# Attention with a routed expert layer on one core: other places for two blocks' gathers and one batch's scatters in GpSimd's queue

## The chip, the cores and the metric

The kernel runs on one core of one Trainium2 chip. Its time is in device microseconds (us) for one execution, and lower is better. Engine names are those of the profile: PE is the matrix engine, DVE the vector engine, ACT the scalar engine, POOL is GpSimd, and SP only issues transfers.

## The reference

Attention with rotary positions over 8 batches of 8 heads, 576 tokens and 64 features is followed by a layer of eight experts, of which each token uses one:

```python
attn = softmax(rotate(q) @ rotate(k).T / 8);  x = (attn @ v) as [4608 tokens, 512]
logits = x @ w_gate + modality_bias[modality_id]
e_idx = argmax(logits, axis=1)
gate_w = softmax(logits)[arange(N), e_idx]
for e in range(8):
    mask = e_idx == e
    h = maximum(x[mask] @ w1[e], 0.0)                 # 512 -> 1024
    out[mask] = gate_w[mask, None] * (h @ w2[e])      # 1024 -> 512
```

All inputs are float32. w1 is [8, 512, 1024] and w2 is [8, 1024, 512].

## The kernel before

**Two parts.** The attention part goes through 32 pairs of heads (`n` = 0 to 31, four pairs to a batch). After the last pair of a batch, `xout(b)` stores the batch's 576 rows of `x` to the scratch tensor `X` in memory, `route(b)` finds each token's expert and its place among that expert's tokens, and `scatter(b, j)`, five indirect DMAs of POOL, writes the tokens' numbers and gate weights into the table `TAB` (line L694 in the profile). The expert part takes the tokens of `TAB` in blocks of 256 rows of one expert, called slots. Slots 0 to 7 hold full blocks from the first five batches, so they can begin while the attention of the last batches still runs; the slots after them wait for every batch.

**A slot's work.** `m_plan` reads the slot's expert and rows into registers, `m_ix` loads its piece of `TAB` as `ix` and `xi` (SP, L930 and L932). `m_gather(s, t, g)` is one indirect DMA of POOL that brings 128 pieces of 128 numbers of `X` into `XG[s % 2][:, t, g, :]` (L956); a slot has eight, four for each half `t`. The first one of a slot is preceded by the POOL instruction that makes its list of rows, `iy` (L948). `m_tr` transposes one half in place on DVE (L1001), `m_tre` splits it into a high part on ACT (L419, `HL<-XG`) and a remainder on DVE (L416, `HL<-XG,HL`). `m_hi` and `m_lo` split the weights in the same way (`W1H`, `W2H` on L419, `W1L`, `W2L` on L416); the loads of weights carry a condition and move data only where a slot's expert differs from the one before it. `m_l1` is the first matrix product (L1020, 96 matmuls to a slot in four groups), `m_l1e` takes it out of PSUM (L1029 on ACT, L1030 on DVE), `m_l2` is the second product (L1043, 24 matmuls to each half), its rows are scaled on ACT (L1046) and scattered to the output by POOL (L1048).

**What sets the order.** PE, ACT, DVE, POOL and, through the first part, SP take their instructions in the order in which the program emits them. Up to the start of the expert part this order comes from a list of jobs, each with a due time: a name's number in `EDGE` or `MOE`, plus 14.438 for every pair of heads, and the list is sorted by it. `MOE["rows"]` holds the due times of the 24 gathers of slots 0, 1 and 2 (eight each), `MOE["ix"]` those of `m_ix`, and `EDGE[27]["SC0"]` that of the first scatter of batch 6, the last batch but one. Jobs due later than `end` (25.0 in the last pair's time) are emitted after the PSUM of the attention part has been given up:

```python
    for s in range(3):
        for i in range(8):
            Z("rows", 8 * s + i, m_gather, s, i // 4, i % 4, AFTER.get((s, i)))
    end = MOE["end"]
    for f in (m_tr, m_tre):
        for t in range(2):
            J(end + 0.05, "moe", z, f, 1, t)
    J(end + 0.1, "moe", z, m_l2, 0, 0)
    jobs.sort(key=lambda t: t[:2])
    cut_ = ([t[0] > PER * z + end for t in jobs] + [True]).index(True)
```

Behind the cut therefore stand slot 1's two `m_tr`, its two `m_tre` and slot 0's first `m_l2`. `chain` goes on from there: slot 0's second `m_l2`, then for each slot its `m_l1`, the next slot's splits and `m_tr`, and its `m_l2`; slot 3's gathers are emitted at slot 1, and so on. Batch 7's routing steps are sprinkled through it by `one()`. An entry of `AFTER` makes a gather wait for a named matmul as well: `('l1', 0)` is the last matmul of slot 0's first product that has been emitted by then.

Each indirect DMA of POOL uses one of eight semaphores in turn and waits until the DMA eight places earlier has landed.

Of the kernel before, what the change touches and what calls it, by code (L numbers as in the profile page):

```python
# [149 lines left out]
        "A_FB": 13.315, "B_FB": 14.059, "AVA": 14.280, "RE": 14.638, "A_F3": 14.844, "B_F3": 15.844, "OTA": 16.826, "AVB": 19.635,  # L150
# [3 lines left out]
    },  # L154
# [41 lines left out]
    setdma=(-353.070, -199.654, -64.082, -129.156),  # L196
    consts=(28.166, 28.282),
    plan=(-34.727, 16.183, -5.857, -25.884),
    ix=(-13.525, 17.418, 11.679, 11.775),
    w1=(-33.501, -27.735, 15.231, -22.655),  # L200
    w2=(-4.011, 1.762, 12.647, -8.483),
    hi=(-22.046, 1.027, 19.870, 16.903),
# [5 lines left out]
    l1=(17.301, 17.002, 22.720, 21.734),  # L208
    l1e=(22.809, 22.869, 24.662, 24.647),
    w1n=(20.502, 24.643, 23.254, 22.825),  # L210
    place=(10.490, 11.490),
    rows=(5.189, -7.595, 2.778, 1.170, -0.984, 8.071, 5.429, 11.766, 24.719, 23.818, 21.468, 24.323, 19.920, 20.117, 22.957, 17.444,
        18.250, 23.228, 17.169, 21.813, 22.941, 24.907, 21.508, 22.829),
    pl=(-114.356, -102.856, -99.906, -88.406, -85.506, -73.956, -51.417, -48.907, -45.303),
    end=25.0,
)
AFTER = {(0, 3): (30, 'av', 0), (0, 4): (30, 'av', 0), (0, 5): (30, 'av', 1), (0, 6): (30, 'av', 1), (0, 7): (30, 'out', 1), (1, 0): ('l1', 0), (1, 1): ('l1', 0), (1, 2): ('l1', 0), (1, 3): ('l1', 0), (1, 4): ('l1', 0), (1, 5): ('l1', 0), (1, 6): ('l1', 0), (1, 7): ('l1', 0)}
PIN = "PE,Activation,DVE,Pool"


# [1 line left out]
def tile_attention_moe(ctx: ExitStack, tc: tile.TileContext, qk, v, mod, wg, mb, w1, w2, rope, cf, ci, out):  # L222
# [912 lines left out]
    def Z(nm, i, f, *a):  # L1135
        J(MOE[nm][i], "moe", z, f, *a)
# [208 lines left out]
```

## Time and profile before

| | us |
|---|---|
| three runs | 919.7, 922.65, 923.22 (median 922.65) |
| the profiled execution | 919.6 |
| its span, first to last instruction | 917.8 |
| PE busy | 859.2 (94% of the span) |
| DVE / ACT / POOL busy | 684.9 / 631.3 / 652.8 |
| matmuls of the expert part from the middle of it on, each slot | 11.20 (L1020) and 11.10 (L1043) |

Times inside the trace are counted from the span's start. In a timeline row the columns are the start, the duration, the engine, the line, the operation with its output and inputs, the count, and in square brackets the engine's idle time before it and what ended it. The granted clock (PEclk) is PE's clock as a share of full speed. The attention part fills the first half; the expert part's matmuls begin at about 469 us and run until the end.

### The profile page before, as it was taken

The page shows a single profiled execution, that of the slowest core. Times are in us where ns is not written, and L with a number is a line of the kernel's source. Part 1 is how long each engine was busy: PE and PEld are TensorE (multiplying, and loading weights), DVE is VectorE, ACT ScalarE, POOL GpSimd, SP SyncE. Part 2 cuts the span into 40 slices and gives each one's busy share as a digit, 9 for nine tenths or more (in the row PEclk, how much of TensorE's full clock was granted, in tenths as well). Part 3 has the DMA queues.
Part 4 walks back from the last instruction along what each step waited for, and adds up shares of the span by engine and source line. Part 5 has one row for each costly group of instructions (what it writes and reads, how often), then busy time and mean ns, then how long its engine had stood idle before and what let it go on. Part 6 is the DMA issues. An engine that isn't in the chain of part 4 may idle for free.

```text
span 917.8 us, 25894 instructions
## 1 busy us (share of the span) xinstructions
PE 859.2 (94%) x9760; PEld 718.8 (78%) x9760; DVE 684.9 (75%) x1516; ACT 631.3 (69%) x1291; POOL 652.8 (71%) x494
## 2 busy tenths in 40 slices
PE   3899999999999999989994899999999999999995
PEld 2776777777777777766683799999999999999995
DVE  7777888888888889877781878766666666666662
ACT  2987988888988988978761555655555555555552
POOL 4989888998889899985466866766666666666400
PEclk9999999999999999999997799999999999999998
DMA  8776768978798887957612921127525112511240
GB/s 270 198 216 159 233 183 204 193 206 202 162 232 184 209 184 206 218 146 195 179 16 38 233 86 41 56 80 236 201 93 185 58 47 93 185 46 38 85 159 15
DMA packets 82466, 136.91 MB, mean 149 GB/s; under 512 B 28795, under 2 KB 53517, under 8 KB 81308
## 3 DMA queue, kind: packets, MB, share of 16 engines
q1 hardware_dynamic: 71740, 114.08, 47.2%
q0 software_dynamic: 9248, 19.46, 7.1%
q8 instruction: 79, 1.29, 0.6%
q10 hardware_dynamic: 1344, 1.62, 0.6%
q14 instruction: 55, 0.45, 0.2%
HBM read 138.16 MB, written 19.51 MB: 172 GB/s over the span
## 4 chain that ended last, share of the span: by engine, by line
PE 50%; issue 2%; POOL 1%; DVE 1%; DMA 1%; ACT 1%; POOLq 0%; DVEq 0%; ACTq 0%
PE psH L1020 22%; PE psY L1043 21%; PE ps L542 3%; PE ps L459 2%; PE ps L482 1%; POOL XG L956 1%; PE ps L1020 1%; DMA TAB<-VAL,oi 1%; PE ps L577 0%; DMA XG<-X,iy 0%; POOL TAB L694 0%; ACT PH L419 0%; DVE HL L416 0%; ACT P L477 0%; DVE X L589 0%
## 5 line engine op out<-in xcount | busy, mean ns | idle before, releaser
L477 ACT ACTIVATE P<-sc,mn 128x576 f32<-128x576 f32 x288 | 219.6, 766 | 5.9 <-DVE mn L468 4.8
L468 DVE CUSTOM_DVE_ANT_1 sc<-ps,ZERO 128x576 f32<-128x576 f32 x288 | 206.5, 748 | 21.8 <-PE ps L459 9.3
L1020 PE MATMUL psH<-HL,W1H 128*128 128x256 f32 x1152 | 205.2, 281 | 15.9 <-ACT W1H L419 15.9
L956 POOL DMA_INDIRECT XG<-X,iy x148 | 178.8, 1208 | 50.1 <-issue 36.7
L1020 PEld LDWEIGHTS psH<-HL,W1H 128*128 128x128 f32 x1152 | 178.9, 190 | 17.9 <-ACT W1H L419 16.4
L459 PE MATMUL ps<-SW 64*128 64x288 f32 x960 | 169.0, 311 | 14.7 <-DMA SW<-HL 12.5
L459 PE MATMUL ps<-HL 64*128 64x288 f32 x960 | 169.5, 311 | 5.8 <-DVE mn L468 2.1
L1020 PE MATMUL psH<-HL,W1L 128*128 128x256 f32 x576 | 162.1, 281 | 0.5 <-DVE W1L L416 0.5
L416 DVE TENSOR_TENSOR W1L<-ST,W1H 128x1024 fp32r<-128x1024 f32 x76 | 90.2, 1221 | 81.7 <-ACT W1H L419 81.6
L459 PEld LDWEIGHTS ps<-SW 64*128 64x128 f32 x960 | 135.5, 189 | 19.2 <-DMA SW<-HL 13.1
L459 PEld LDWEIGHTS ps<-HL 64*128 64x128 f32 x960 | 135.7, 189 | 11.3 <-issue 5.7
L542 PE MATMUL ps<-PH,V 128*64 128x320 f32 (+1 forms) x1024 | 138.2, 412 | 3.4 <-ACT P L477 2.1
L1048 POOL DMA_INDIRECT out_dram<-sc,ix x36 | 43.7, 1213 | 115.9 <-ACT sc L1046 100.0
L482 PEld LDWEIGHTS ps<-idf,P 64*128 64x128 f32 x2624 | 96.3, 139 | 33.3 <-ACT P L477 12.4
L1043 PE MATMUL psY<-W2L,SW 128*128 128x512 f32 (+1 forms) x304 | 118.0, 388 | 0.0
L1043 PE MATMUL psY<-W2H,SW 128*128 128x512 f32 (+1 forms) x304 | 116.7, 384 | 0.0
L482 PE MATMUL ps<-idf,P 64*128 64x64 f32 x2624 | 108.9, 226 | 7.5 <-ACT P L477 3.5
L516 DVE COPY PH<-ps 128x512 f32<-128x512 f32 (+1 forms) x160 | 98.4, 630 | 17.4 <-PE ps L482 12.2
L1020 PEld LDWEIGHTS psH<-HL,W1L 128*128 128x128 f32 x576 | 109.5, 190 | 0.8 <-DVE W1L L416 0.8
L436 POOL TENSOR_TENSOR HL<-ST,HL 128x1152 fp32r<-128x1152 f32 x31 | 82.4, 2657 | 38.9 <-ACT HL L419 38.8
L542 PEld LDWEIGHTS ps<-PH,V 128*64 128x64 f32 x1024 | 69.5, 136 | 50.3 <-issue 5.2
L419 ACT ACTIVATE PH<-ps 128x512 f32<-128x512 f32 (+1 forms) x160 | 85.5, 551 | 33.4 <-PE ps L482 25.4
(200 smaller groups left out, 1578.3 us busy)
## 6 DMA issues: line engine op xcount, KB each, us to landing
ST<-in_moe_w_dram SPq DMA_DIRECT2D x152, 512.0 KB
ST<-in_qk_dram SPq DMA_DIRECT2D x62, 576.0 KB
SW<-HL SPq DMA_DIRECT2D x124, 216.0 KB
V<-in_v_dram SPq DMA_DIRECT2D x32, 256.0 KB
X<-X SPq DMA_DIRECT2D x8, 1024.0 KB
XG<-X,iy POOLq DMA_INDIRECT x148, 3.1
V<-in_v_dram SPq DMA_DIRECT2D x64, 16.0 KB
X<-XT SPq DMA_DIRECT2D x16, 64.0 KB
```

What stands on the lines that cost most here:

```text
L416: nc.vector.tensor_tensor(o, a, b, op=ALU.subtract)
L419: return nc.scalar.activation(o, i, AF.Copy, scale=scale)
L436: e.tensor_tensor(d["HL"][:, 1, o], a, d["HL"][:, 0, o].bitcast(F32), op=ALU.subtract)
L459: nc.tensor.matmul(ps[:, g, 0:288], t[:, wq, q0:q0 + P], t[:, wk, k0:k0 + 288], start=(m == 0), stop=(m == len(L) - 1))
L468: nc.vector.tensor_tensor_reduce(sc, d.pop(("S", u))[:, :, 0:288], ZERO.unsqueeze(2).to_broadcast([P, 2, 288]), 1.0, FMAX, ALU.add, ALU.mi ...
L477: nc.scalar.activation(p, sc.rearrange("p a b -> p (a b)"), AF.Exp, bias=mn, scale=-1.0, accum_out=d["sum"][:, u:u + 1])
L482: nc.tensor.transpose(ps[:, g, c:c + 64], src[r, k0:k0 + P], idf[r, r])
L516: mine.append((nc.vector.tensor_copy if g else acopy)(o, i).ins)
L542: i = nc.tensor.matmul(pa[hh * 64:hh * 64 + 64, 0:c1 - c0], d["V"][:, hh, kt, :], r, start=(kt == 0), stop=(kt == 4))
L956: inst = nc.gpsimd.indirect_dma_start(out=XG[s % 2][:, t, g, :], out_offset=None, in_=X.rearrange("n (i f) -> (n i) f", f=P)[0:rows], in_o ...
L1020: l1_[s] = nc.tensor.matmul(ps[:, i, :], w[:, c, f0:f0 + P], x[:, c, :], start=(m == 0), stop=(m == 11)).ins
L1043: nc.tensor.matmul(ps, hx[:, c, t * P:(t + 1) * P], x[:, c, h * w:h * w + w], start=(m == 0), stop=(m == 23))
```

## The change

The due times are changed, and eight waits are left out:

- Slot 1's eight gathers get the due times 17.36 to 17.43 in their order, so that they stand in one run behind the first two scatters of batch 5. They waited for matmuls of slot 0's first product; that wait goes (the eight entries of `AFTER`).
- Slot 2's eight gathers get 25.15 to 25.22, and batch 6's first scatter 25.30 in the last pair's time (83.052 in its own). All nine are then behind the cut, so they are emitted after slot 1's `m_tr` and `m_tre` and slot 0's first `m_l2`.
- Slot 1's `m_ix` goes from 17.418 to 17.300, so that it still stands ahead of its gathers.

```diff
-        "RK11": 71.745, "RK12": 78.963, "RK13": 82.481, "RK14": 82.519, "SC0": 82.645,
+        "RK11": 71.745, "RK12": 78.963, "RK13": 82.481, "RK14": 82.519, "SC0": 83.052,
...
-    ix=(-13.525, 17.418, 11.679, 11.775),
+    ix=(-13.525, 17.300, 11.679, 11.775),
...
-    rows=(5.189, -7.595, 2.778, 1.170, -0.984, 8.071, 5.429, 11.766, 24.719, 23.818, 21.468, 24.323, 19.920, 20.117, 22.957, 17.444,
-        18.250, 23.228, 17.169, 21.813, 22.941, 24.907, 21.508, 22.829),
+    rows=(5.189, -7.595, 2.778, 1.170, -0.984, 8.071, 5.429, 11.766, 17.360, 17.370, 17.380, 17.390, 17.400, 17.410, 17.420, 17.430,
+        25.150, 25.160, 25.170, 25.180, 25.190, 25.200, 25.210, 25.220),
...
-AFTER = {(0, 3): (30, 'av', 0), ..., (0, 7): (30, 'out', 1), (1, 0): ('l1', 0), ..., (1, 7): ('l1', 0)}
+AFTER = {(0, 3): (30, 'av', 0), ..., (0, 7): (30, 'out', 1)}
```

The order on PE, DVE and ACT is the same before and after. On POOL, in the stretch from batch 5's first two scatters to slot 0's second output scatter, the program has this before (`XG_76` is `XG[1]`, which slot 1 uses, `XG_75` is `XG[0]`, slot 2's; `TAB<-VAL,oi` is a scatter of routing results):

```order
L948 TENSOR_SCALAR iy<-xi,CF 128x8
L956 DMA XG_76<-X,iy 128x128
L956 DMA XG_75<-X,iy 128x128
L956 DMA XG_76<-X,iy 128x128 x2
L694 DMA TAB<-VAL,oi 41472x2
L956 DMA XG_76<-X,iy 128x128
L956 DMA XG_75<-X,iy 128x128 x2
L694 DMA TAB<-VAL,oi 41472x2
L956 DMA XG_75<-X,iy 128x128 x2
L956 DMA XG_76<-X,iy 128x128
L956 DMA XG_75<-X,iy 128x128
L956 DMA XG_76<-X,iy 128x128 x3
```

Ahead of these rows stand slot 2's `iy`, one gather of slot 2 and a scatter; behind them one scatter of batch 6, slot 2's last gather, the first output scatter, and batch 6's other four. The program after the change has this on POOL from the same place on:

```order
L948 TENSOR_SCALAR iy<-xi,CF 128x8
L956 DMA XG_76<-X,iy 128x128 x8
L694 DMA TAB<-VAL,oi 41472x2 x3
L683 CAST oi<-of 128x5
L1048 DMA out_dram<-sc,ix 4608x512
L948 TENSOR_SCALAR iy<-xi,CF 128x8
L956 DMA XG_75<-X,iy 128x128 x8
L694 DMA TAB<-VAL,oi 41472x2 x5
L1048 DMA out_dram<-sc,ix 4608x512
```

Slot 1's gathers now stand together and ahead of three scatters; slot 2's stand together behind slot 0's first output scatter. On SP the order of batch 7's `xout` and of slot 4's `m_ix` is exchanged; both stand ahead of the loads of slot 2's W1. The rows of the difference are:

```order
-L930 ISA
-L930 DMA ix<-TAB 128x4
-L932 ISA
-L932 DMA xi<-TAB 128x1x16
-L601 DMA X<-XT 64x8x32
 L599 DMA X<-X 128x2048
-L601 DMA X<-XT 64x8x32
+L601 DMA X<-XT 64x8x32 x2
+L930 ISA
+L930 DMA ix<-TAB 128x4
+L932 ISA
+L932 DMA xi<-TAB 128x1x16
```

So slot 4's `ix` and `xi` now come behind the stores of batch 7's rows of `X`.

More of the change, by code (lines that the diff above doesn't have):

```diff
@@ L216 @@
 )
-AFTER = {(0, 3): (30, 'av', 0), (0, 4): (30, 'av', 0), (0, 5): (30, 'av', 1), (0, 6): (30, 'av', 1), (0, 7): (30, 'out', 1), (1, 0): ('l1', 0), (1, 1): ('l1', 0), (1, 2): ('l1', 0), (1, 3): ('l1', 0), (1, 4): ('l1', 0), (1, 5): ('l1', 0), (1, 6): ('l1', 0), (1, 7): ('l1', 0)}
+AFTER = {(0, 3): (30, 'av', 0), (0, 4): (30, 'av', 0), (0, 5): (30, 'av', 1), (0, 6): (30, 'av', 1), (0, 7): (30, 'out', 1)}
 PIN = "PE,Activation,DVE,Pool"
```

## The prediction

> **What bounds the kernel now.** I read the page first, for the engine with the highest share and for the slices in which it drops.
>
> ```profile
> PE 859.2 (94%) x9760; PEld 718.8 (78%) x9760; DVE 684.9 (75%) x1516; ACT 631.3 (69%) x1291; POOL 652.8 (71%) x494
> PE   3899999999999999989994899999999999999995
> PEclk9999999999999999999997799999999999999998
> ```
>
> PE is the bound, and its one weak place past the beginning is around slices 21 to 23 of 23 us each, where its clock falls too. PE's timeline there has one hole, from the last matmul of slot 0 to the first of slot 1:
>
> ```profile
> 492.06 0.39 PE L1043 MATMUL psY<-W2L,SW 128*128 128x512 f32 x1
> 508.37 0.58 PE L1020 MATMUL psH<-HL,W1H 128*128 128x256 f32 x1 [15.92 <-ACT W1H L419]
> ```
>
> The chain that ended last says what fills it (start, duration, what):
>
> ```profile
> 498.23 2.56 DMA XG<-X,iy
> ...
> 500.92 0.72 DVE XG L1001
> ...
> 501.71 1.12 ACT HL L419
> 502.86 2.08 DVE HL L416 x2
> ...
> 507.26 1.06 ACT W1H L419
> 508.35 1.24 DVE W1L L416
> ...
> 509.63 8.15 PE psH L1020 x46
> ...
> 517.93 5.71 PE psH L1020 x48
> 523.64 11.10 PE psY L1043 x48
> 534.74 11.20 PE psH L1020 x96
> ```
>
> Slot 1's last gather is issued at 498.23 and landed at 500.8. Then come transposes, the split of the rows, and the split of the weights, which ACT and DVE do only behind the rows. ACT names W1H as the releaser, but that was late because the gathers were. From 523.64 PE goes in blocks of 11.1 and 11.2 without a hole, to the end, so whatever makes slot 1 start and run earlier is taken off the end in full as long as slot 2 is not late in its turn.
>
> A slower clock makes the hole dearer (columns: PE, PEld, DVE, ACT, POOL busy, granted clock, DMA share, GB/s):
>
> ```profile
> 392.28:395.69 3.41, 1.81 (x22) 1.25 (x20) 2.34 (x8) 0.95 (x3) 2.71 (x7) 1.00 0.56 161
> 395.69:399.10 3.41, 3.41 (x58) 2.61 (x56) 3.41 (x10) 2.82 (x6) 1.57 (x1) 1.00 0.01 5
> 491.26:494.68 3.42, 1.19 (x6) 0.63 (x4) 0.00 (x0) 0.00 (x0) 2.51 (x4) 1.00 0.37 32
> 494.68:515.16 20.48, 6.33 (x28) 6.03 (x29) 12.74 (x25) 8.90 (x13) 14.71 (x15) 0.50 0.57 100
> ```
>
> After 3.4 us in which PE was busy for 1.19, the clock is 0.50 until 515.16; after 3.4 us with 1.81 it stayed at 1.00.
>
> **The change, first part: slot 1's gathers.** POOL's rows from slot 2's list of rows on, some left out:
>
> ```profile
> 467.92 1.35 POOL L948 TENSOR_SCALAR iy<-xi,CF 128x8 int32<-128x8 int32 x1
> 469.54 1.09 POOL L956 DMA_INDIRECT XG<-X,iy  x1 [0.28 <-POOL iy L948]
> 470.94 5.23 POOL L694 DMA_INDIRECT TAB<-VAL,oi  x1 [0.31 <-issue]
> 476.27 0.27 POOL L948 TENSOR_SCALAR iy<-xi,CF 128x8 int32<-128x8 int32 x1
> ...
> 479.54 2.57 POOL L956 DMA_INDIRECT XG<-X,iy  x1 [0.30 <-issue]
> ...
> 485.05 1.03 POOL L956 DMA_INDIRECT XG<-X,iy  x1 [0.30 <-issue]
> ...
> 498.23 1.00 POOL L956 DMA_INDIRECT XG<-X,iy  x1 [0.30 <-issue]
> ```
>
> POOL is never idle here for more than the 0.3 between two DMAs: the gathers are late because slot 2's seven and three scatters stand among them, not because of the wait for matmuls. That wait I cost at nothing: it was over before POOL came to it. In the changed order the list made at 467.92 is slot 1's, and its eight gathers take the next eight DMA places, those at 469.54, 470.94 and so on to 485.05; the second `iy` (0.27 and its gaps) drops out between. The last one starts at 485.05 instead of 498.23, if two long durations stay where they are. They belong to the first of these DVE rows:
>
> ```profile
> 470.60 1.21 DVE L416 TENSOR_TENSOR W1L<-ST,W1H 128x1024 fp32r<-128x1024 f32 x1
> 471.73 1.21 DVE L416 TENSOR_TENSOR W2L<-ST,W2H 128x1024 fp32r<-128x1024 f32 x1
> ...
> 474.07 1.21 DVE L416 TENSOR_TENSOR W2L<-ST,W2H 128x1024 fp32r<-128x1024 f32 x1
> ...
> 478.88 2.34 DVE L416 TENSOR_TENSOR W2L<-ST,W2H 128x1024 fp32r<-128x1024 f32 x2
> ...
> 500.92 1.30 DVE L1001 STREAM_TRANSPOSE XG<-XG 128x512 f32<-128x512 f32 x2 [17.64 <-DMA XG<-X,iy]
> ```
>
> The DMA of 470.94 began during the first subtraction and ended at 476.17, 0.89 after the last (475.28); that of 479.54 ended at 482.11, 0.89 after 481.22. A DMA of POOL that starts while DVE subtracts takes its usual time only after it. DVE's order is unchanged and nothing ahead of these rows moves, so I keep both stalls. The Trainium skill (SBUF — State Buffer, section "Who interferes with whom") says that a DVE instruction with two SBUF inputs blocks a GpSimd instruction that reads SBUF, and also that descriptor generation was seen not to be stalled by `tensor_tensor`, since it writes. By the second sentence the gathers would run unstalled, which is the first rival below; the row with 5.23 agrees with the first one, because an indirect DMA reads its list.
>
> The eighth gather then lands here after:
>
> ```profile
> L956 POOL DMA_INDIRECT XG<-X,iy x15: 1003/1012/2567, 469.5 to 498.2; - x15
> ...
> DMA to landing us min/median/max: 2.6/2.8/4.9
> ```
>
> I take 2.6, the price of the row at 498.23 (2.56), since now no scatter stands among the eight; 4.9 is the other end. That is 487.65, so the second transpose starts at 487.8. The first one needs only the first four gathers, which are out by 478.9 and landed by about 482, before DVE is free (500.92 less its 17.64 of idle time, 483.3); its ACT part is done early as well. Before, both halves waited for the end. From the second transpose: 0.67 for it, ACT's high part 1.1, DVE's remainder 1.1 with about 0.1 between, so DVE is through at 490.75, and as before (504.94 to 508.37) PE's first matmul comes 3.43 later, at 494.2. ACT's scaling of slot 0's first half, which stands ahead of W1H on ACT, needs PE's 24 matmuls up to 486.9 (half of 11.10 before 492.45) and is no longer late. PE's hole becomes 492.45 to 494.2, 1.75 instead of 15.92.
>
> Before, slot 1's first product took 508.37 to 523.64, 15.27. At full clock it costs 1.24 for the first piece of W1L behind the first two matmuls, then 94 of 96 matmuls by the 11.20 row, 10.97, and 0.15 for batch 7's small matmuls in it (509.63 + 8.15 to 517.93): 12.36. It ends at 506.56. The gain is 523.64 − 506.56 = 17.1, of which 14.2 are the hole and 2.9 the clock.
>
> Is the clock safe? PE idles 1.75 and then up to 1 more for W1L, so its busy time in a stretch of 3.41 is between 0.9 and 1.7, between the two rows above (1.19 fell, 1.81 did not). A fall to 0.50 for one such stretch costs half of it, 1.7 at most. I take half of that, 0.8, and keep 0 and 1.7. The Trainium skill (TensorE: Matmul & The Clock Gate, "What's actually happening") puts the fall after one idle window of 3.4 us; by it there is no fall and the sum stays at 17.1. The row with 1.19 busy, where the clock fell, differs from a wholly idle window.
>
> **Second part: slot 2's gathers**, now behind slot 0's first output scatter, which waits for ACT. The cover is slot 1's 22 us of matmuls. For the price I take what POOL did beside the same DVE work before:
>
> ```profile
> 504.46 1.37 POOL L1048 DMA_INDIRECT out_dram<-sc,ix  x1 [2.38 <-ACT sc L1046]
> 506.14 1.00 POOL L694 DMA_INDIRECT TAB<-VAL,oi  x1 [0.30 <-issue]
> ...
> 518.74 1.01 POOL L956 DMA_INDIRECT XG<-X,iy  x1 [0.30 <-issue]
> ...
> L956 POOL DMA_INDIRECT XG<-X,iy x8: 1003/1408/2053, 514.1 to 526.2; - x8
> ...
> DMA to landing us min/median/max: 6.4/6.5/7.0
> ```
>
> The first DMA behind the output scatter started at 506.14, the eighth at 518.74, with an `iy` between, as in the new order. Everything there moves up by 14.2 with DVE, so the scatter runs from 490.3 (three routing scatters of 1.3 from 486.4 fill POOL until then), and the eighth gather starts at about 504.5. With the weight loads beside it, it lands after 6.4 to 7.0, at 511.5 at the latest. It has to land by:
>
> ```profile
> 527.93 1.26 DVE L1001 STREAM_TRANSPOSE XG<-XG 128x512 f32<-128x512 f32 x2
> ...
> 530.88 1.09 DVE L416 TENSOR_TENSOR HL<-XG,HL 128x512 fp32r<-128x512 f32 x1
> ```
>
> From transposes to split rows are 4.04. PE wants slot 2 at 506.56 + 11.10 = 517.66, so 513.6 is the limit and 2.1 are left. I cost it at nothing; if the cover is gone, this run is what is late next.
>
> **The rest.** POOL's queue holds the same instructions as before; what is put off are batch 5's last three scatters and batch 6's five, by up to 16, and only the table loads of slot 8 and later read them. Slot 0's second output scatter and slot 3's gathers come at about 513 and 515 to 528, the gathers nearly as before (514.1 to 526.2), while PE's need of slot 3 moves up to 540 (517.66 and one block of 22.3): landed by 535, 1 us before its limit of 536. On SP the exchange lets slot 4's two loads wait for DVE's last values of batch 7; their reader is POOL at about 530, so nothing.
>
> Sum: 17.1 less 0.8 is 16.3. From the profiled 919.6 that is 903.3; this execution lay 3.05 below the median of the three runs, and from 922.65 it is 906.35. I say 905, between the two.
>
> **The rivals.**
>
> 1. The gathers are not held by DVE (the stalled DMA of 470.94 slips through between subtractions). Each takes 1.31, the eighth starts by 478.7 and slot 1 is ready before PE is: no hole, all of 15.92 + 3.9 = 19.8 gone, 903 from the median. For it: the subtractions are separate instructions, and one handover that POOL catches frees up to 3.5; against it: the same DMA place waited through all of them.
> 2. Slot 2 is late. Eight gathers at the dearest of 2.05 + 0.3 end at 511, plus 7.0 is 518: PE stalls 4.5 and the clock falls for 1.7 or more. The gain is 10 to 11, the time 912. For it: the margin of 2.1; against it: the median 1.41 of such gathers.
> 3. The change doesn't reach PE: another input of W1H is as late as the gathers (the values of the last pair, which DVE takes behind the split rows). Then 919 to 922. Against it: POOL's rows without idle time, and DVE idle for 17.64 before its transposes, with nothing but the gathers to wait for.
> 4. Slower: slot 2's run, now behind the output scatter, makes a longer hole than the one removed. It decides from a landing later than 513.6 + 17.1 = 530.7, that is (530.7 − 7.0 − 492.2) / 7 = 4.5 from gather to gather; at 5 it would be 926. One row has that length (5.23), with subtractions back to back; of the eight of 514.1 to 526.2, beside the DVE work that it would meet, none took over 2.05.
>
> **How the numbers follow.** The forecast has 0.73, the rivals 0.10, 0.10, 0.04 and 0.03. About 0.5%, 4.6 us, is what a measurement of this kernel can tell from no change. The forecast's own range is 902.5 (17.1 off the profiled execution) to 909.5 (landing after 4.9 and a full fall of the clock, so 13.1 off the median). With rival 2 it reaches to 912.5, with the first to 900: 900 to 912.5. Faster by more than 0.5% takes the forecast and both first rivals, 0.92; rival 3 is the same, 0.05; slower 0.03.
>
> **What would show it.** Right: in the changed trace eight gathers in a row from 469.5 to about 486, with long ones at the second and fifth; transposes apart, at 483 and 488; PE's first `psH` at 494 and the next `psY` at 506 to 508; no hole before slot 2. Wrong: a hole ahead of slot 2's or slot 3's L1020 with gathers landing just before, or W1H on ACT still near 507.

## The result and the profile after

The changed kernel takes 908.13 us (median of four runs, 905.53 to 910.39) against 922.13 (four runs, 919.7 to 923.22) for the kernel before beside it: a ratio of 0.9851, with an interval of 0.9815 to 0.9887. That is 14.0 us less; forecast were 905 and a range of 900 to 912.5. The profiled execution took 909.4, its span is 907.6, against 919.6 and 917.8 before. Two more comparisons below, each on another chip, gave ratios of 0.9891 and 0.9825. The ratios leave out runs over 1.5% above the fastest of their kernel, which are six of the twelve of `ahead_timed` below and none of the others.

Shares and slices on the page hardly tell the two apart: PE has 2 us more busy time, 95% of a shorter span, and the dips of work and clock in slices 21 to 23 are gone.

```profile
PE 861.3 (95%) x9760; PEld 719.0 (79%) x9760; DVE 684.5 (75%) x1516; ACT 631.7 (70%) x1291; POOL 649.2 (72%) x494
PEclk9999999999999999999999999999999999999998
```

PE's timeline shows what is left of the hole: 1.61 in front of slot 1's first matmuls and 0.76 for the first piece of W1L, where 15.92 and 0.46 were.

```profile
496.30 0.39 PE L1043 MATMUL psY<-W2L,SW 128*128 128x512 f32 x1
498.30 0.50 PE L1020 MATMUL psH<-HL,W1H 128*128 128x256 f32 x2 [1.61 <-ACT W1H L419]
499.56 0.58 PE L1020 MATMUL psH<-HL,W1L 128*128 128x256 f32 x1 [0.76 <-DVE W1L L416]
```

POOL's rows are the eight gathers of slot 1 in one run, with long ones at the second and fifth place:

```profile
472.17 1.33 POOL L948 TENSOR_SCALAR iy<-xi,CF 128x8 int32<-128x8 int32 x1
473.78 1.10 POOL L956 DMA_INDIRECT XG<-X,iy  x1 [0.28 <-POOL iy L948]
475.18 5.24 POOL L956 DMA_INDIRECT XG<-X,iy  x1 [0.31 <-issue]
...
483.34 3.00 POOL L956 DMA_INDIRECT XG<-X,iy  x1 [0.30 <-issue]
...
489.26 1.01 POOL L956 DMA_INDIRECT XG<-X,iy  x1 [0.30 <-issue]
```

and on DVE the two transposes stand apart, the second behind the landing of the last gather (the first row is the last of the four subtractions that held the gather of 475.18):

```profile
478.31 1.21 DVE L416 TENSOR_TENSOR W2L<-ST,W2H 128x1024 fp32r<-128x1024 f32 x1
...
487.44 0.70 DVE L1001 STREAM_TRANSPOSE XG<-XG 128x512 f32<-128x512 f32 x1
491.82 0.71 DVE L1001 STREAM_TRANSPOSE XG<-XG 128x512 f32<-128x512 f32 x1 [3.69 <-DMA XG<-X,iy]
```

The chain that ended last still leads from this gather through the transpose and the two splits to PE, and then along PE in blocks of about 11.2 to the end:

```profile
489.26 2.54 DMA XG<-X,iy
...
491.82 0.72 DVE XG L1001
...
492.62 1.13 ACT HL L419
...
493.77 1.11 DVE HL L416
...
497.19 1.06 ACT W1H L419
...
498.28 1.24 DVE W1L L416
...
499.56 6.98 PE psH L1020 x46
...
506.69 5.71 PE psH L1020 x48
512.40 11.20 PE psY L1043 x48
```

**Where the 10.2 between the two spans come from.** "The stretch" is from the end of slot 0's last L1043 matmul to the start of slot 1's first. It was 31.03 (492.45 to 523.48) and is 15.55 (496.69 to 512.24): 15.48 gained. Two things went against it in this execution. The expert part's first matmul started at 473.14 instead of 468.90, 4.24 later, with the order of the attention part unchanged; a gap of PE of 2.55 at 251.3 in the first half is part of it. And from slot 1's second product to the end it took 395.39 instead of 394.35, 1.04 longer; a slot's 48 second products took 11.20 instead of 11.10, which alone would be 1.8 over the 18 slots from slot 1 on. 15.48 less 4.24 and 1.04 is 10.2. The start of the expert part differs as much between executions of one kernel: 468.90 and 477.13 (`before_again`) for the kernel before, 473.14, 476.71 (`after_again`) and 467.86 (`after_third`) for the changed one. The medians, in which the start of the expert part averages out in part, differ by 14.0.

### The profile page after: what moved, and what is told of

Read it like the earlier page. It is cut to its first block, busy times and chain, and to the rows that moved or that the text cites. A ratio compares the mean times of both kernels' runs of the same rounds, so it can differ in the third digit from the quotient of the medians.

```text
span 907.6 us, 25897 instructions
## 1 busy us (share of the span) xinstructions
PE 861.3 (95%) x9760; PEld 719.0 (79%) x9760; DVE 684.5 (75%) x1516; ACT 631.7 (70%) x1291; POOL 649.2 (72%) x494
## 4 chain that ended last, share of the span: by engine, by line
PE 49%; issue 2%; POOL 1%; ACT 1%; DVE 1%; DMA 0%; POOLq 0%; ACTq 0%; DVEq 0%
PE psH L1020 22%; PE psY L1043 22%; PE ps L542 2%; PE ps L459 2%; PE ps L482 1%; POOL XG L956 1%; DMA XG<-X,iy 0%; PE ps L577 0%; ACT PH L419 0%; ACT P L477 0%; DVE X L589 0%; POOL TAB L694 0%; POOL iy L948 0%; DVE W1L L416 0%; ACT HL L419 0%
## 5 line engine op out<-in xcount | busy, mean ns | idle before, releaser
L956 POOL DMA_INDIRECT XG<-X,iy x148 | 186.1, 1257 | 50.1 <-issue 36.6
L1020 PE MATMUL psH<-HL,W1H 128*128 128x256 f32 x1152 | 203.9, 280 | 1.6 <-ACT W1H L419 1.6
L1020 PEld LDWEIGHTS psH<-HL,W1H 128*128 128x128 f32 x1152 | 177.8, 189 | 3.6 <-ACT W1H L419 2.0
L1020 PE MATMUL psH<-HL,W1L 128*128 128x256 f32 x576 | 161.4, 280 | 0.8 <-DVE W1L L416 0.8
L1048 POOL DMA_INDIRECT out_dram<-sc,ix x36 | 46.7, 1298 | 105.6 <-ACT sc L1046 62.9
L1043 PE MATMUL psY<-W2L,SW 128*128 128x512 f32 (+1 forms) x304 | 119.8, 394 | 0.0
L1043 PE MATMUL psY<-W2H,SW 128*128 128x512 f32 (+1 forms) x304 | 117.3, 386 | 0.0
L1020 PEld LDWEIGHTS psH<-HL,W1L 128*128 128x128 f32 x576 | 109.0, 189 | 1.0 <-DVE W1L L416 1.0
```

What stands on the lines that cost most here:

```text
L956: inst = nc.gpsimd.indirect_dma_start(out=XG[s % 2][:, t, g, :], out_offset=None, in_=X.rearrange("n (i f) -> (n i) f", f=P)[0:rows], in_o ...
L1020: l1_[s] = nc.tensor.matmul(ps[:, i, :], w[:, c, f0:f0 + P], x[:, c, :], start=(m == 0), stop=(m == 11)).ins
L1043: nc.tensor.matmul(ps, hx[:, c, t * P:(t + 1) * P], x[:, c, h * w:h * w + w], start=(m == 0), stop=(m == 23))
```

## The experiments

The expectations call slot 0's last and slot 1's first second product by the same stretch. The time to slot 0's last matmul is the same 23.55 in before and after, counted from the first L1020, so that places are compared as distances from that first L1020. A place is one DMA in POOL's queue, 1.31 from start to start where nothing holds it; a window is one of the steps of 3.41 in which the clock changes (last section). The table puts the runs together: where slot 1's eighth gather starts, how long PE's hole in front of slot 1 is, the stretch, for how long the clock was at 0.5 in or near it, and the time (of a single run where no number of runs stands).

| run | eighth gather, from the first L1020 | hole | stretch | clock 0.5 | time | before beside it |
|---|---|---|---|---|---|---|
| before | 29.33 | 15.92 | 31.03 | 20.48 | 922.13 (4) | |
| after | 16.12 | 1.61 | 15.55 | 3.41 | 908.13 (4) | 922.13 (4) |
| first_only | 17.43 | 2.93 | 17.10 | 3.41 | 905.04 | 921.65 |
| second_only | 20.12 | 6.69 | 21.06 | 6.83 | 911.41 | 921.65 |
| wait_kept | 17.43 | 2.91 | 18.00 | 6.83 | 905.53 | 921.65 |
| run_ahead | 10.21 | none | 11.30 | none | 903.81 | 921.65 |
| no_sub2 | 11.58 | none | 11.30 | none | 901.84 | 923.30 |
| slot2_late | 16.12 | 1.84 | 15.98 | 3.41 | 906.48 | 923.30 |
| ev_early | 16.12 | 3.53 | 18.49 | 6.83 | 907.11 | 923.30 |

Single times do not order these runs: the first L1020 started anywhere from 467.3 to 473.1 in them, without a tie to the edit, so the stretch is what each is judged by.

**Slot 1's half alone** (`first_only`, from the kernel before: the waits out, slot 1's gathers and `m_ix` moved, slot 2's gathers and the scatter left):

```diff
-    ix=(-13.525, 17.418, 11.679, 11.775),
+    ix=(-13.525, 17.300, 11.679, 11.775),
...
-    rows=(5.189, -7.595, 2.778, 1.170, -0.984, 8.071, 5.429, 11.766, 24.719, 23.818, 21.468, 24.323, 19.920, 20.117, 22.957, 17.444,
+    rows=(5.189, -7.595, 2.778, 1.170, -0.984, 8.071, 5.429, 11.766, 17.360, 17.370, 17.380, 17.390, 17.400, 17.410, 17.420, 17.430,
...
-AFTER = {(0, 3): (30, 'av', 0), ..., (0, 7): (30, 'out', 1), (1, 0): ('l1', 0), ..., (1, 7): ('l1', 0)}
+AFTER = {(0, 3): (30, 'av', 0), ..., (0, 7): (30, 'out', 1)}
```

> Only slot 1's half of the change: its eight gathers in one run and without their waits; slot 2's gathers and batch 6's first scatter keep the due times of before, so that slot 2's list of rows, one gather of it and slot 1's own list stand ahead of the run. Measured by PE's stretch from slot 0's last matmul to slot 1's first L1043, which was 31.03 us before and 15.55 after the change. Theory (PE waits for the DMA place of slot 1's eighth gather and for nothing else): one DMA more ahead, so the eighth gather starts about 1.3 later than after the change, PE's first psH too, and the stretch is 16.9, up to 18.5 if the clock falls for a second 3.4 us. Rival (the gain comes from slot 2's gathers being out of the way altogether, or from their transfers): the stretch stays above 20.

The stretch is 17.10. One `iy` and one gather of slot 2 still stand ahead of slot 1's run; here the `iy` was held by DVE instead of the gather (469.15, for 4.71), and the eighth gather is one DMA place, 1.31, later than in the changed kernel. So is PE. Slot 1's half alone brings 13.9 of the 15.5.

**Slot 2's half alone** (`second_only`, from the kernel before: only slot 2's gathers and batch 6's scatter are put off):

```diff
-        "RK11": 71.745, "RK12": 78.963, "RK13": 82.481, "RK14": 82.519, "SC0": 82.645,
+        "RK11": 71.745, "RK12": 78.963, "RK13": 82.481, "RK14": 82.519, "SC0": 83.052,
...
-        18.250, 23.228, 17.169, 21.813, 22.941, 24.907, 21.508, 22.829),
+        25.150, 25.160, 25.170, 25.180, 25.190, 25.200, 25.210, 25.220),
```

> Only slot 2's half of the change: its gathers and batch 6's first scatter go behind slot 0's first output scatter; slot 1's gathers keep the due times and the waits for slot 0's first product that they had before, and share POOL with three scatters only. Theory (the place of the eighth gather): it is the eleventh DMA from the same point, with the first gather held for PE until the middle of slot 0's first product, so it starts about 4 us later than after the change; the stretch is 19.5, or up to 21.5 with a longer fall of the clock. That is, either half alone gives three quarters of the gain or more, since both only take other DMAs out from between slot 1's gathers. Rival (slot 1's run without the waits is what counts): the stretch stays near 31.

The stretch is 21.06, so taking slot 2's gathers out of slot 1's way brings 10.0 by itself. Here the wait that `AFTER` makes is not free any more. POOL's timeline:

```profile
471.07 0.27 POOL L948 TENSOR_SCALAR iy<-xi,CF 128x8 int32<-128x8 int32 x1
476.44 1.10 POOL L956 DMA_INDIRECT XG<-X,iy  x1 [5.09 <-issue]
...
480.47 2.53 POOL L694 DMA_INDIRECT TAB<-VAL,oi  x1 [0.30 <-issue]
...
489.90 1.00 POOL L956 DMA_INDIRECT XG<-X,iy  x1 [0.30 <-issue]
```

POOL stood for 5.09 ahead of the first gather, with nothing to do. The row names no releaser; the gather started 6.66 after the first L1020, and 6.65 after it in `wait_kept` below, the other run in which this wait shows, so it goes with PE's progress. Two halves that bring 13.9 and 10.0 alone bring 15.5 together: both clear the same queue.

**The wait kept** (`wait_kept`, the changed kernel with the eight entries back):

```diff
+AFTER = {..., (1, 0): ('l1', 0), (1, 1): ('l1', 0), ..., (1, 7): ('l1', 0)}
```

> The changed kernel with one thing put back: slot 1's gathers again wait for the matmuls of slot 0's first product. Theory: before, this wait was over when POOL came to it, but in the new order POOL comes to it early, so the first gather is held from 0.3 behind the list until the middle of slot 0's first product (some 5 us), where DVE's subtractions held the second gather anyway. One DMA place is lost: the stretch is 16.9 instead of 15.55. Rival 1 (the wait costs nothing in either order): 15.5. Rival 2 (the wait costs its whole length of 5): 20.5.

```profile
474.84 1.10 POOL L956 DMA_INDIRECT XG<-X,iy  x1 [6.27 <-issue]
...
478.89 2.50 POOL L956 DMA_INDIRECT XG<-X,iy  x1 [0.30 <-issue]
...
485.62 1.01 POOL L956 DMA_INDIRECT XG<-X,iy  x1 [0.30 <-issue]
```

POOL waits 6.27 for slot 0's first matmuls, and still only one place is lost (17.43 instead of 16.12): while it waits, the DVE subtractions that would have held its second gather for 5.24 pass by. The hole is 1.30 longer. The stretch is 2.45 longer, neither the 16.9 of the theory nor a rival's number, as the clock was down for two windows instead of one.

**Further ahead** (`run_ahead`, the changed kernel with slot 1's `ix` and gathers 2.2 units of due time earlier and its plan 1.1, ahead of batch 5's scatters):

```diff
-    plan=(-34.727, 16.183, -5.857, -25.884),
-    ix=(-13.525, 17.300, 11.679, 11.775),
+    plan=(-34.727, 15.050, -5.857, -25.884),
+    ix=(-13.525, 15.100, 11.679, 11.775),
...
-    rows=(5.189, -7.595, 2.778, 1.170, -0.984, 8.071, 5.429, 11.766, 17.360, 17.370, 17.380, 17.390, 17.400, 17.410, 17.420, 17.430,
+    rows=(5.189, -7.595, 2.778, 1.170, -0.984, 8.071, 5.429, 11.766, 15.200, 15.210, 15.220, 15.230, 15.240, 15.250, 15.260, 15.270,
```

> The changed kernel with slot 1's run (and its loads of the table) ahead of batch 5's first two scatters instead of behind them. Theory (the place of the eighth gather, and DVE's subtractions): two DMAs fewer ahead, so the gather that DVE holds for about 5 us is a later one of the run; the eighth starts about 6 us earlier than after the change or is the one held until 0.9 after the second pair of subtractions, and lands before slot 0's second product ends. PE has no hole there, the clock does not fall, and the stretch is 11.4 to 12.0 instead of 15.55. Rival (W1H and W1L of slot 1, or the values of the last pair on DVE, are as late as the gathers): the stretch stays above 14.

The hole is gone, the clock stays up and the stretch is 11.30, with slot 1's matmuls right behind slot 0's:

```profile
494.35 0.40 PE L1043 MATMUL psY<-W2L,SW 128*128 128x512 f32 x1
494.59 0.40 PE L1020 MATMUL psH<-HL,W1H 128*128 128x256 f32 x2
```

**No subtractions beside the gathers** (`no_sub2`, the changed kernel; the first four W2L pieces there are set to zero instead of computed, so the part of that expert's second product that uses them is left out):

```diff
-            sub(W2[1][:, sl, :], ST2[:, sl, :], W2[0][:, sl, :].bitcast(F32))
+            nc.vector.memset(W2[1][:, sl, :].bitcast(F32), 0.0) if skip and skip.pop() else sub(...)
...
-    late = []
+    late, skip = [], [1] * 4
```

> The changed kernel, with slot 0's four subtractions for W2L on DVE replaced by fills with zero of the same tiles (so slot 0 leaves the small remainder of w2 out); DVE's other instructions and every order stay. Tested is what holds two of slot 1's gathers on POOL for 5.24 and 3.00 us. Theory (a DVE subtraction, which reads two tiles of SBUF, holds a DMA of POOL that starts during it until 0.9 after its end): the second gather is held by one W1L subtraction only, 1.8 us, the third by another, about 2, the fifth not at all; the eighth starts some 4.4 us earlier, PE has no hole, and the stretch from slot 0's last matmul to slot 1's first L1043 is 11.3 to 11.5 instead of 15.55. Rival (what holds them is not the subtraction: the landing of an earlier DMA, PE's progress, or writing of any kind by DVE): the long durations and the stretch stay, 15 to 17.

POOL's rows from the second gather on, and DVE's two subtractions that are left and its memsets:

```profile
472.09 1.68 POOL L956 DMA_INDIRECT XG<-X,iy  x1 [0.31 <-issue]
474.07 1.89 POOL L956 DMA_INDIRECT XG<-X,iy  x1 [0.31 <-issue]
476.27 1.01 POOL L956 DMA_INDIRECT XG<-X,iy  x1 [0.30 <-issue]
...
481.50 1.00 POOL L956 DMA_INDIRECT XG<-X,iy  x1 [0.30 <-issue]
```

```profile
471.66 1.21 DVE L416 TENSOR_TENSOR W1L<-ST,W1H 128x1024 fp32r<-128x1024 f32 x1
473.03 0.91 DVE L993 MEMSET W2L<- 128x1024 f32 x1 [0.16 <-issue]
...
473.91 1.17 DVE L416 TENSOR_TENSOR W1L<-ST,W1H 128x1024 fp32r<-128x1024 f32 x1
...
480.13 0.91 DVE L993 MEMSET W2L<- 128x1024 f32 x1 [0.16 <-issue]
481.21 0.91 DVE L993 MEMSET W2L<- 128x1024 f32 x1 [0.16 <-issue]
```

The 5.24 and the 3.00 are gone. What is held, 1.68 and 1.89, stands beside the two subtractions that are left and ends 0.9 after each; the gathers beside the last two memsets take 1.0. The eighth gather comes 4.54 sooner (11.58 instead of 16.12), and the hole is gone.

**Slot 2's gathers later** (`slot2_late`, the changed kernel with due times of 65.150 to 65.220, so that they stand behind batch 6's five scatters as well, at 501.60 to 512.66):

```diff
-        25.150, 25.160, 25.170, 25.180, 25.190, 25.200, 25.210, 25.220),
+        65.150, 65.160, 65.170, 65.180, 65.190, 65.200, 65.210, 65.220),
```

> The changed kernel with slot 2's list and eight gathers behind batch 6's five scatters instead of ahead of them, so about 7 us later. It measures the margin of slot 2. Theory (PE wants slot 2's rows split when slot 1's second product ends; by the prediction 2.1 us are left over, and the run lands 7 us later): a new hole of 3 to 6 us opens ahead of slot 2's first L1020, the clock falls, and what the change brought shrinks by 4 to 8 us. Rival (slot 2's gathers land sooner than the prediction took, since the changed trace shows no wait for them): hole under 1.5 us, or none, and the time within 2 us of the changed kernel's. Slot 1's stretch stays at 15 to 17 in both.

```profile
519.00 0.71 DVE L1001 STREAM_TRANSPOSE XG<-XG 128x512 f32<-128x512 f32 x1 [3.90 <-DMA XG<-X,iy]
...
520.90 1.09 DVE L416 TENSOR_TENSOR HL<-XG,HL 128x512 fp32r<-128x512 f32 x1
```

```profile
521.07 0.28 PE L1020 MATMUL psH<-HL,W1H 128*128 128x256 f32 x1
522.05 0.38 PE L1020 MATMUL psH<-HL,W1H 128*128 128x256 f32 x1 [0.71 <-DVE HL L416]
```

This is the hole that my forecast named as next, and it is 0.71 long, under the 3 to 6 of the theory. Without it the eighth gather might start at 511.95; in the changed kernel slot 2's first matmul starts at 523.44 instead of 521.07, so its limit is about 514.3, and its eighth gather starts at 508.18. The margin is some 6.

**Batch 7's last values ahead of the transposes** (`ev_early`, the changed kernel; DVE and ACT do them earlier, so that less stands between slot 1's rows and W1H):

```diff
-        23.807, "OUT": 24.531,
+        23.807, "OUT": 24.531, "RI": 24.800, "EVB": 24.850, "EVA": 24.900,
```

> The changed kernel with the last pair's division and its stores out of PSUM (RI, EVA, EVB of pair 31, some 1.9 us of DVE) ahead of slot 1's transposes instead of behind them, where DVE now idles for 3.7 us. SP's stores of batch 7's rows of X then also start some 8 us earlier. Theory (behind the eighth gather the path to PE is a chain of DVE and ACT work, of which 1.9 is the last pair's values): the stretch gets shorter by the hole, from 15.55 to 12 to 13.5, with no fall of the clock or a short one. Rival (the earlier stores of X delay the landing of slot 1's last gathers, by as much or more): the stretch stays at 15.5 or gets longer.

The hole grew to 3.53. The eighth gather keeps its place, and its rows arrive later: issued at 485.91, it had landed only at 493.01, 7.10 after. Its transpose:

```profile
493.03 0.71 DVE L1001 STREAM_TRANSPOSE XG<-XG 128x512 f32<-128x512 f32 x1 [6.45 <-DMA XG<-X,iy]
```

and on SP the stores of `X`, which these values release, now go out from 485.13 to 487.85, beside that gather:

```profile
485.13 0.70 SPq L601 DMA_DIRECT2D X<-XT  x1
485.92 0.56 SPq L599 DMA_DIRECT2D X<-X  x1
486.58 1.27 SPq L601 DMA_DIRECT2D X<-XT  x1
```

In the changed kernel they go out behind its landing, from 496.40. The DMA view tells what moved: in `ev_early` SP's transfers (queue q1) moved 1.19 MB between 481 and 495, which is the three stores (1.18 MB) and two small loads of the table; the loads of weights issued there, which carry a condition, moved nothing. That these stores delay the gather is therefore the likely reading; no run moved them alone.

**Again, and the variant without a hole, on two other chips** (unchanged copies; `ahead_timed` and `ahead_third` are `run_ahead`).

> The kernel before once more, for what differs from run to run without a change. Theory: the attention part's length to the first matmul of slot 0 (468.90 us in the profile before, 473.14 after the change, 467.3 to 471.2 in the variants) differs by some us in a kernel that is the same, so the 4.2 by which the profiled execution of the change came later to slot 0 are not the change's; the stretch from slot 0's last matmul to slot 1's first L1043 is again 31.0 within 0.5. Rival: attention takes 468.9 again within 0.5 and is lengthened by the change.

> The changed kernel once more, timed in five rounds. Theory: the stretch is 15.5 within 0.5 if the clock falls for one stretch of 3.4 us behind PE's hole, 16.5 if for two, 14 if for none; the time is 14 to 15.5 us under the kernel before (the stretch's 15.5 less up to 1.8 that the second products of a slot may take longer). Rival: the gain of a median of five rounds is near 10, as the two profiled executions differ, and attention is longer with the change.

> Slot 1's run ahead of batch 5's scatters, timed in five rounds beside the changed kernel. Theory: no hole for PE between slots 0 and 1, no fall of the clock, stretch 11.3, so 4.2 us under the changed kernel and 18 to 20 under the kernel before. Rival: the table's rows are written later or X's rows are stored earlier, something behind is late in turn, and the time is that of the changed kernel.

> The changed kernel again, unchanged, beside the kernel before and beside the variant with slot 1's gathers further ahead. Theory (the gain is the hole of PE between slots 0 and 1): a ratio of 0.984 to 0.990 to the kernel before, a stretch of 15.5 to 18.0 us between slot 0's last and slot 1's first second product. Rival (the gain hangs on the chip it was seen on): a ratio above 0.995.

> Slot 1's gathers ahead of slot 0's last work, so that PE has no hole between slots 0 and 1. Theory: the stretch is 11.3 us, 4 to 6 us less than with the change, and the ratio to the kernel before is 0.4 to 0.7% lower than the changed kernel's. Rival (the further 4 us are lost again in the expert part, where PE had gaps of 6 to 10 us without a cause that the trace shows): a ratio no lower than the changed kernel's, with such gaps in the slots after it.

| run | median us (range, runs) | ratio to before | interval | hole | stretch |
|---|---|---|---|---|---|
| before_again | 928.14 (924.11 to 931.43, 17, taken beside all three) | | | 15.86 | 31.00 |
| after_again | 918.08 (914.22 to 923.32, 6) | 0.9891 | 0.9858 to 0.9924 | 2.88 | 17.04 |
| ahead_timed | 924.14 (909.69 to 939.95, 12); 921.03 for the six of the ratio | 0.9911 | 0.9872 to 0.9950 | none | 14.85 |
| after_third | 903.84 (901.87 to 905.77, 5), before 920.05 | 0.9825 | 0.9802 to 0.9849 | 1.58 | 15.72 |
| ahead_third | 900.16 (899.35 to 902.11, 5), before 920.05 | 0.9793 | 0.9771 to 0.9814 | none | 11.29 |

On the last chip everything came as the earlier traces had it: the change is worth 16.2, the variant without a hole another 3.7, and its stretch is 4.43 shorter. On the chip of the first three rows both gained less, and the variant, against its expectation, no more than the changed kernel. The 10.1 of the changed kernel is the number of the rival there, but not its reason, as the attention part was no longer than before (476.71 and 477.13 to the first L1020). From slot 1's second product to the end `after_again` took 400.13 and `ahead_timed` 400.03, against 394.12 in `before_again`. PE had gaps there, inside the expert part, that wait for nothing the profile shows, and the kernel before did not have them on this chip; the timeline of `ahead_timed`:

```profile
531.01 0.28 PE L1020 MATMUL psH<-HL,W1H 128*128 128x256 f32 x1 [0.80 <-issue]
532.47 0.28 PE L1020 MATMUL psH<-HL,W1L 128*128 128x256 f32 x1 [0.82 <-issue]
...
533.90 0.28 PE L1020 MATMUL psH<-HL,W1L 128*128 128x256 f32 x1 [0.42 <-issue]
```

The ones at 507.0 to 509.8 are inside the stretch, which is why it is 14.85 there and not 11.3, and both groups were followed by a window at half clock. `after_again` had such gaps at 561.1 to 564.4, followed by two. Its longer hole of 2.88 is something else: DVE held a scatter for 4.07 and then slot 1's first gather for 5.59, and the eighth gather came 17.49 after the first L1020, about one place later than in after. I take the gaps to belong to that chip or that hour, as no profiled execution on the other chips had them, but each kernel was profiled there only once; what they wait for stays open, and so does whether the variant beats the changed kernel on every chip. It did on the last chip; in the first, single run it lay 17.8 under the kernel before, and the changed kernel 14.0 in its own comparison; on the chip with the gaps it was no faster.

## Why the prediction was right, point by point

- **POOL's order sets slot 1's start.** Right. Over the runs of the table a place of 1.31 for the eighth gather is 1.3 of hole (16.12 to 17.43, 1.61 to 2.93). From 29.33 to 16.12 it is 14.31 for 13.21; the other 1.1 is the first half's transpose and split, which no longer stand behind the last gather, as forecast. `second_only` has the same 1.1, with both transposes in a row after 492.6.
- **The hole.** 1.75 was forecast, 1.61 measured. The landing, taken at 2.6 and not 4.9, was 2.54. Both stalls stayed: 5.24 and 3.00, forecast from 5.23 and 2.57.
- **The clock.** The step that was mis-sized. I took half of a full fall, 0.8; the clock fell for a whole window, and slot 1's first product took 14.10 (498.30 to 512.40) where 12.36 was worked out at full clock. That is 1.74 more, most of it in this window: 46 matmuls took 6.98, the next 48 took 5.71. From slot 0's last matmul to the end of this product, as the prediction counts, it is 15.71 (496.69 to 512.40) where my terms gave 14.1 without a fall and 14.9 with the half. After's windows show it at 1.57 busy, between the two rows I had:

```profile
495.62:499.03 3.41, 1.57 (x7) 0.85 (x5) 2.77 (x8) 2.29 (x4) 2.74 (x4) 1.00 0.87 231
499.03:502.44 3.41, 2.88 (x13) 2.88 (x14) 3.34 (x8) 3.41 (x6) 2.50 (x3) 0.50 0.88 161
```

  The Trainium skill (TensorE: Matmul & The Clock Gate, "What's actually happening") puts the fall after one idle window; the runs here disagree, as PE was at 46% in this one. The rule from the skill would have given no fall, and so would have missed by 1.6.
- **The removed wait.** Costed at nothing, and in the old order it was nothing: by the 6.65 of `wait_kept` it was over at 475.55, and slot 1's first gather started at 476.81. In the new one it would cost 1.3 of hole and a second window at half clock, 2.45 of the stretch (`wait_kept`): it was the change of order that made it matter.
- **Slot 2.** Costed at nothing, rightly; the margin of 2.1 was really some 6.0. Of the 3.9, 1.7 are PE's later need (519.36 instead of 517.66, both counted from before's start of the expert part), 1.3 the earlier landing (508.18 and 6.3, taken from `slot2_late`, instead of a last landing after 7.0), and 0.9 the path behind it, 3.1 in `slot2_late` instead of 4.04, since only the second half stands behind the last gather.
- **Slot 3.** Its gathers ran from 518.15 to 527.72, PE had no hole there. Right.
- **The sum.** 16.3 was forecast and 15.5 came in the stretch, 0.8 less for the clock. From the median of before, 922.13, the sum gives 905.8 and 908.13 was measured, 2.3 more. Of these 0.8 are the clock and 1.0 is what the profiled execution lost behind the stretch, with its second products at 11.20; the 0.5 left is less than the spread of the start of the expert part.
- **The rivals.** The first (gathers not held) fell with the 5.24, and `no_sub2` shows what it would have brought: a stretch 19.7 shorter than before, where 19.8 was worked out. Of the two sentences of the Trainium skill named there (SBUF — State Buffer, "Who interferes with whom") the runs agree with the first, and these gathers do not behave by the second: beside DVE subtractions with two SBUF inputs an indirect DMA was held until 0.9 after their end (475.18 + 5.24 against 478.31 + 1.21), beside memsets it took its 1.0. The second, slot 2 late, would have needed a landing 6.0 later. The third fell with W1H, which followed the gathers. The fourth would have needed 4.5 from gather to gather; the dearest of slot 2's started 2.37 before the next (502.45 and 504.82).

## What to carry to other kernels

Where, as here, an in-order queue is never idle and another engine waits for its last item, count the places of that queue: what a needed item gains is the number of places it moves up, times the spacing, and two edits that clear the same places do not add up. A wait in an old order that costs nothing may cost something in the new one, and the other way round, so each is priced again in the order in which it will stand. Before a load is moved forward, ask also what is in the air beside it: beside stores that were let go earlier, a gather's landing took 7.1 us instead of 2.5 (`ev_early`).

## What the runs showed of the hardware

- **The clock decides in fixed windows.** In every execution all falls and rises lie on one grid of 3.41 us over the whole span. Of the windows at full clock between 60 and 890 us of the fourteen profiled executions, those in which PE was busy for less than 1.56 (of 3.41) were all followed by half clock; of the seven between 1.56 and 1.59 four were and three weren't. Above that only three were, at 1.78, 1.97 and 2.25, the last two beside the unexplained gaps. By this count a hole of some 1.9 (3.41 less 1.56) costs about 1.6 more if it lies in one window, as in after, and may cost nothing if it is split between two: in `second_only` the window in which the hole began had 1.77 busy and was not followed by a fall, the next one, wholly idle, was. A window at half clock is followed by full clock if PE was busy all through it; with 2.81 and 2.88 busy (after) that was so too, with 2.93 (`wait_kept`) it was not, nor with 2.92 and 2.95 in the two traces of the kernel before.

```profile
491.21:494.62 3.41, 0.53 (x3) 0.10 (x1) 2.68 (x10) 1.54 (x4) 2.58 (x5) 1.00 0.59 197
494.62:498.04 3.42, 2.93 (x12) 2.63 (x13) 3.34 (x7) 3.42 (x5) 2.81 (x3) 0.50 0.97 244
```

- **Second products come in two speeds.** A slot's 48 took 11.10 in some executions and 11.20 in others, all through an execution and with no tie to the kernel: `after_again` went like before, after and `after_third` at the slower pace. Over the 18 slots from slot 1 on that is 1.8 us; the cause is open.
